# A fused attention and softplus feed-forward kernel: another list and order of the start, and strided scores of 54 rows in two lasting PSUM tiles

## The chip, the core and the metric

The kernel runs on one core of a Trainium2 chip. The metric is the device time of one execution in microseconds. TensorE (PE; its weight loads are listed as PEld) multiplies matrices into PSUM, VectorE (DVE), ScalarE (ACT) and GpSimd (POOL) work on elements, and SyncE (SP) issues most DMAs. The engines have a queue each and meet through semaphores.

## The reference

Eight batches of eight heads attend over 576 tokens of 64 dimensions; the first four heads see the last 32 keys, the other four the keys of their own class modulo 32. The result, as rows of 512 numbers, goes through a feed-forward layer with a softplus.

```python
scores = scale * np.matmul(q, k.transpose(0, 1, 3, 2))
mask_local = (rel >= 0) & (rel < stride)                    # heads 0 to 3
mask_strided = (rel >= 0) & (pos[None, :] % stride == pos[:, None] % stride)
attn = softmax(np.where(masks, scores, -1e9))
x = (attn @ v) as (4608, 512)
h = x @ w_in                                                # 512 -> 2048
g = np.maximum(h, 0.0) + np.log1p(np.exp(-np.abs(h)))
out = g @ w_out                                             # 2048 -> 512
```

The host reorders the strided heads so that the 18 tokens of a class lie side by side; a group of three classes is 54 tokens.

## The kernel before

**The feed-forward part.** The 4608 tokens are taken in nine chunks of 512 and the 2048 hidden channels in 16 slices f of 128, so there are 144 steps. A step has one *hidden* block on TensorE (`hidden`, L729): 12 matmuls of 128 x 128 by 512, since each of four pairs of heads gives three products, high part of x by high and by low part of w_in, and low part of x by high part. They add up in one PSUM bank. ACT takes absolute value, exponential and logarithm of it (`log_part`, L741 to L746), DVE adds the positive part (`softplus`, L750, tile `u`), which is the last reader of the bank, and splits the sum into a high and a low part (`gh` at L269, `gl` at L762). Two steps later an *output* block (`output`, L769) of 12 matmuls adds to four PSUM banks `py`, one for each 128 tokens. After the 16th slice `result` copies the four banks out and stores them.

**The attention part.** Two heads make a pair, in each batch in the order local, strided, local, strided; 32 pairs in all. The first four go through a form of their own at the start. Each of the other 28 has a *visit* on TensorE (`visit`): a row of small matmuls with its scores and with the weighted sums of the pair before it. The scores of a strided pair (`late_scores`, L422) are 22 products, 11 groups by two heads, which the profile lists as 44 loads and 44 matmuls. `lhsT` is 64 columns of q, the group's 54 and the first 10 of the next, so 64 rows of PSUM are written for each head; the rows of the surplus mean nothing. They fill two banks. `add_mask` (L533) reads the banks, and DVE and ACT make the softmax in SBUF (prob). Weighted sums are L475 for a local pair, L461 for a strided one, scores of local pairs L443.

**The banks.** PSUM has eight: four for `py`, one each in the pools `ps_s` and `ps_o`, and two in the pool `ps_h` with `bufs=2`. From `ps_h` come the banks of the hidden blocks, of the strided scores (both), of a third of the local scores and of the transposes in the start. The pool hands them out in turn, each after the last use of the tile that had it before.

**The order.** All is issued by hand. `FIRST` is a list of some 500 names that sets the order of the start: loads (q, k, v, wi, wo), scores S, maxima X, exponentials E, transposes T and their copies C, weighted sums V, copies into x (H, the high part) and differences (L, the low part), the preparation of the weights (a, B, d, h, l), the hidden blocks F and output blocks O of the first chunk, its softplus parts A, u, Gh, Gl, and the visits J4 to J8. W is a pair of matmuls without use that keep TensorE going. `ON_POOL`, `ON_VECTOR` and `ON_SCALAR` say which names run on another engine than the usual one, `WIDE` which halves of the first pairs take their exponential in one piece over SBUF, where the others take it in pieces of 64 columns straight from PSUM. Behind the list a planner (`Plan`) places the rest: each task has an urgency, an engine, a cost and tasks it follows; a task is put at the first gap of its engine after the end of what it follows, and all are issued in order of their start. There `F`, `O`, `S` and `Y` are hidden block, output block, visit and mask.

Of the kernel before, what the change touches and what calls it, by code (L numbers as in the profile page):

```python
# [44 lines left out]
ao0 v0 X10 hi0 r0 wi9 x10 R0 M0 S20 T02 Bo0 do0 C02 x11 v1 T00 T01 v2 S21 E10 wi1 X20 li0 E11 C01
C00 S30 ho0 V00 r1 Y20 X21 wi3 R1 x21 E20 S31 v3 V02 E21 Z20 wi2 M1 T11 X30 V01 X31 Y30 H00 q4 r2
C11 R2 L00 lo0 x31 T12 E30 M2 T10 H01 k4 Z30 L01 ai9 C12 E31 V11 T20 C10 Bi9 V12 wo6 V10 r3 T22 C20
H10 di9 T21 R3 L10 wo1 H11 wi4 C22 wo2 L11 M3 V22 C21 ai1 V20 V21 H20 Bi1 di1 T32 hi1 C32 H21 T31
wo3 ai3 L20 C31 L21 Bi3 T30 C30 V32 ai2 di3 li1 V31 V30 H30 H31 hi3 Bi2 wi6 L30 D4 L31 Fa0 di2 wi8
wo4 hi9 ao6 J4 Y42 Y40 v4 hi2 F0 li3 li2 W18 wi10 wi5 ao1 A0 Bo1 Y41 Ae0 Fa1 Al0 wi7 ai4 do1 q5 wo15  # L50
li9 Bo6 F1 wo8 u0 wi13 Gh0 ho1 Km A1 wo10 Bi4 lo1 Ae1 ao3 F2 Gl0 di4 wo5 Al1 hi4 O0 A2 do6 X4 u1 ho6
F3 lo6 ai6 Bi6 Gh1 li4 ao2 Ae2 s4 wo13 Bo2 Al2 Gl1 ai8 di6 Bo3 Bi8 do3 E4 u2 hi6 Z4 r4 do2 k5 ho3
di8 R4 li6 O1 Gh2 A3 Ae3 Al3 M4 F4 u3 Gl2 wi11 P41 ho2 lo2 Gh3 Gl3 F6 O2 A4 wi14 ai5 Ae4 wi12 P40
Al4 lo3 ai7 A6 hi8 P42 Bi5 ao4 Bi7 Kz di5 D5 u4 hi5 Ae6 P43 O3 Al6 u6 Gh4 Gh6 J5 v5 k7 di7 li8 li5
Bo4 ai11 ao5 Y51 wo14 Y50 F5 X5 H40 Gl4 wo7 hi7 Bi11 k6 do4 A5 s5 ho4 E5 Bo5 lo4 li7 Ae5 F9 Z5 ai10
wo11 r5 Al5 wo12 Gl6 di11 R5 wo9 q6 A9 Ae9 Bi10 O4 u5 ao8 di10 M5 do5 Gh5 Al9 hi11 hi10 u9 Gl5 F7
ho5 P53 A7 lo5 F8 H41 Bo8 L40 Ae7 Gh9 P51 ao7 Gl9 wi15 Al7 D6 O5 li10 A8 P50 do8 u7 P52 Ae8 ai12 O6
L41 ho8 Al8 Bo7 J6 u8 li11 v6 F10 Gh7 ai13 Y60 do7 Gh8 H51 Y61 lo8 Gl8 ho7 q7 Y62 X6 Bi12 lo7 H50
Gl7 F11 ao9 A10 di12 s6 ao10 Ae10 hi12 Bi13 Al10 Bo10 di13 u10 A11 O7 li12 E6 ai14 L50 hi13 F12 Z6
r6 Bo9 Ae11 do9 ho9 Bi14 R6 M6 Al11 do10 L51 li13 u11 D7 lo9 O8 Gh11 ho10 F13 ao13 Gh10 P60 Gl11 A12  # L60
O9 P62 di14 P63 Gl10 k8 hi14 Ae12 li14 P61 ao11 A13 Al12 lo10 u12 Ae13 Al13 Gh12 ao12 u13 ai15 Bo11
do11 J7 Bo12 Y71 do12 H61 Y70 O10 X7 Gh13 H60 v7 Gl12 Bo13 ho11 lo11 W23 s7 do13 E7 ho12 Bi15 F14 Z7
r7 A14 lo12 di15 R7 hi15 L61 L60 M7 ao15 li15 Ae14 q8 ho13 D8 P72 Al14 k9 P71 Gl13 lo13 P70 u14 O11
# [60 lines left out]
def attention_softplus_ffn(  # L124
# [406 lines left out]
    def add_mask(n, j):  # L531
        pv, sv, _ = parts(n, j)
        nc.vector.tensor_tensor(pv, sv, mask_of(n, j), op=ALU.add)  # L533
# [599 lines left out]
```

## Time and profile before

| | us |
|---|---|
| median of three runs | 878.86 (878.12 to 880.0) |
| the profiled execution | 880.72 |
| its span, first to last instruction | 878.9 |
| TensorE busy | 863.3 |
| DVE busy | 590.4 |
| ACT busy | 395.5 |

In a row of the page's groups or of the timeline stand line, engine, operation, tile written <- tiles read, shapes, and the time in us; in brackets the engine's idle time just before, and what ended it. In a row of the waits stand who waited, for whom, the total, how often and the longest. TensorE's granted clock is 0.998 of full speed over the span.

### The profile page before, as it was taken

The page shows a single profiled execution, that of the slowest core. Times are in us where ns is not written, and L with a number is a line of the kernel's source. Part 1 is how long each engine was busy: PE and PEld are TensorE (multiplying, and loading weights), DVE is VectorE, ACT ScalarE, POOL GpSimd, SP SyncE. Part 2 cuts the span into 40 slices and gives each one's busy share as a digit, 9 for nine tenths or more (in the row PEclk, how much of TensorE's full clock was granted, in tenths as well). Part 3 has the DMA queues.
Part 4 walks back from the last instruction along what each step waited for, and adds up shares of the span by engine and source line. Part 5 has one row for each costly group of instructions (what it writes and reads, how often), then busy time and mean ns, then how long its engine had stood idle before and what let it go on. Part 6 is the DMA issues. An engine that isn't in the chain of part 4 may idle for free.

```text
span 878.9 us, 16412 instructions
## 1 busy us (share of the span) xinstructions
PE 863.3 (98%) x6704; PEld 706.5 (80%) x6704; DVE 590.4 (67%) x1282; ACT 395.5 (45%) x703; POOL 75.4 (9%) x97
## 2 busy tenths in 40 slices
PE   7999999999999999999999999999999999999998
PEld 4788888888788878888788878888788888888886
DVE  5999968777876777768685867677776533333332
ACT  5877735444444443443444444344443333333332
POOL 4566650000000000000000000000000000000000
PEclk9999999999999999999999999999999999999999
DMA  9975103111210121102211121012100010001001
GB/s 305 345 274 188 48 14 103 49 50 43 90 42 22 49 75 42 43 28 56 76 43 42 43 90 43 15 47 85 41 16 16 1 48 1 1 1 48 1 1 48
DMA packets 46465, 56.46 MB, mean 64 GB/s; under 512 B 3322, under 2 KB 31670, under 8 KB 46390
## 3 DMA queue, kind: packets, MB, share of 16 engines
q1 hardware_dynamic: 46102, 55.09, 19.5%
q8 instruction: 52, 0.85, 0.4%
q10 hardware_dynamic: 288, 0.33, 0.2%
q14 instruction: 23, 0.19, 0.1%
HBM read 45.97 MB, written 9.44 MB: 63 GB/s over the span
## 4 chain that ended last, share of the span: by engine, by line
PE 95%; ACT 2%; DVE 2%; issue 1%; DMA 1%; SPq 0%; POOL 0%; DVEq 0%; ACTq 0%
PE ph L729 45%; PE py L769 44%; PE ps L422 1%; PE ps L461 1%; PE ps L443 1%; PE ps L475 1%; DMA early_h<-in_qk_dram 1%; DVE u L750 1%; ACT u L744 1%; ACT u L746 1%; ACT u L741 0%; PE pv L622 0%; PE py L393 0%; PE po L443 0%; PE po L461 0%
## 5 line engine op out<-in xcount | busy, mean ns | idle before, releaser
L769 PE MATMUL py<-w_o,gh 128*128 128x512 f32 x1152 | 357.8, 392 | 0.0
L729 PE MATMUL ph<-x_h,w_i 128*128 128x512 f32 x1152 | 355.6, 390 | 1.0 <-DVE prob L533 0.5
L741 ACT ACTIVATE u<-ph 128x512 f32<-128x512 f32 x144 | 86.1, 598 | 376.0 <-PE ph L729 375.7
L729 PEld LDWEIGHTS ph<-x_h,w_i 128*128 128x128 f32 x1152 | 215.6, 188 | 47.0 <-DVE u L750 1.1
L769 PEld LDWEIGHTS py<-w_o,gh 128*128 128x128 f32 x1152 | 214.3, 188 | 44.8
L769 PE MATMUL py<-w_o,gl 128*128 128x512 f32 x576 | 224.2, 389 | 0.0
L729 PE MATMUL ph<-x_l,w_i 128*128 128x512 f32 x576 | 224.1, 389 | 0.0
L750 DVE SCALAR_TENSOR_TENSOR u<-ph,u 128x512 f32<-128x512 f32 x144 | 99.2, 689 | 181.6 <-ACT u L746 180.1
L769 PEld LDWEIGHTS py<-w_o,gl 128*128 128x128 f32 x576 | 108.1, 188 | 22.7
L729 PEld LDWEIGHTS ph<-x_l,w_i 128*128 128x128 f32 x576 | 108.1, 188 | 22.6
L762 DVE TENSOR_TENSOR gl<-u,gh 128x512 fp32r<-128x512 f32 x135 | 93.4, 692 | 10.9 <-PE po L475 0.5
L746 ACT ACTIVATE u<-u 128x512 f32<-128x512 f32 x144 | 91.0, 632 | 4.3
L744 ACT ACTIVATE u<-u 128x512 f32<-128x512 f32 x144 | 91.0, 632 | 4.3
L592 DVE STREAM_TRANSPOSE masks_pt<-prob 32x160 f32<-32x160 f32 x224 | 70.1, 317 | 3.9
L269 DVE CAST gh<-u 128x512 fp32r<-128x512 f32 x129 | 54.6, 424 | 8.6 <-PE py L769 0.5
L580 DVE STREAM_TRANSPOSE pt_groups<-prob 32x192 f32<-32x192 f32 (+1 forms) x112 | 39.6, 354 | 3.1
L580 DVE STREAM_TRANSPOSE masks_pt<-prob 32x160 f32<-32x160 f32 (+1 forms) x112 | 39.6, 354 | 3.1
L548 ACT ACTIVATE prob<-prob 128x576 f32<-128x576 f32 (+1 forms) x28 | 19.4, 693 | 46.2 <-DVE prob L542 46.2
L269 ACT COPY qT<-prob 128x576 f32<-128x576 f32 x27 | 34.5, 1279 | 6.0 <-PE ps L422 5.2
L552 DVE TENSOR_REDUCE st<-prob 128x9 f32<-128x576 f32 (+1 forms) x28 | 21.2, 758 | 9.2 <-ACT prob L548 9.2
L533 DVE TENSOR_TENSOR prob<-ps,masks_pt 128x320 f32<-128x320 f32 (+1 forms) x28 | 10.8, 390 | 24.6 <-PE ps L443 14.5
L269 DVE COPY o<-py 128x512 f32<-128x512 f32 (+1 forms) x16 | 10.7, 670 | 16.9 <-PE py L769 16.9
(105 smaller groups left out, 587.1 us busy)
## 6 DMA issues: line engine op xcount, KB each, us to landing
out_dram<-o SPq DMA_DIRECT2D x35, 256.0 KB, 2.0
ri<-in_moe_w_in_dram SPq DMA_DIRECT2D x16, 512.0 KB, 9.8
ro<-in_moe_w_out_dram SPq DMA_DIRECT2D x16, 512.0 KB, 6.8
prob<-in_qk_dram SPq DMA_DIRECT2D x28, 288.0 KB, 2.8
kT<-in_qk_dram SPq DMA_DIRECT2D x28, 288.0 KB, 3.4
v_in<-in_v_dram SPq DMA_DIRECT2D x14, 162.0 KB
v_in<-in_v_dram SPq DMA_DIRECT2D x14, 160.0 KB, 3.1
v_in<-in_v_dram SPq DMA_DIRECT2D x14, 128.0 KB, 3.1
```

The costliest lines, as they stand in the source:

```text
L269: (engine.copy if engine is nc.scalar else engine.tensor_copy)(dst, src)
L548: nc.scalar.activation(pv, pv, AF.Exp, scale=SCALE)
L552: nc.vector.tensor_reduce(sm, pv, axis=AX.X, op=ALU.add)
L580: nc.vector.transpose(dst[:, :, :32], src[:, :, :32])
L592: nc.vector.transpose(pt_late[lo : lo + 32, h, windows, col : col + 32], src[:, :, 32 * c : 32 * c + 32],)
L729: nc.tensor.matmul(ph, lhsT=w32["i", f][:, half, cc * P : (cc + 1) * P], rhs=x_of(x, cc)[:, t0 : t0 + n], start=(i == 0), stop=(i == 3 * N ...
L741: nc.scalar.activation(us[c, f], phs[c, f], AF.Abs)
L744: nc.scalar.activation(u, u, AF.Exp, scale=-1.0)
L746: nc.scalar.activation(u, u, AF.Ln, bias=1.0)
L750: nc.vector.scalar_tensor_tensor(u, in0=phs.pop((c, f)), scalar=0.0, in1=u, op0=ALU.max, op1=ALU.add)
L762: engine.tensor_tensor(g, us.pop((c, f)), ghs[c, f].bitcast(F32), op=ALU.subtract)
L769: nc.tensor.matmul(py[t], lhsT=g[:, sl], rhs=w32["o", f][:, half], start=(f == 0 and n == 0), stop=(f == NFC - 1 and n == 2),)
```

## The change

The score products of strided pairs take 54 columns of q, so that they write 54 rows per head; the ten columns of zeros behind qT are cleared no longer. The pool of two turning PSUM buffers becomes two tiles that last for the whole kernel, `free_banks`. `take_bank` takes the one that was left first, and `leave_bank` gives it back, at the softplus, at the added mask and at the copy of an early transpose. In the planner, a task may follow another with a lead, and the visit of a strided pair now follows, besides what it did, the softplus of its step with a lead of 0.7 and the output block two steps back. The list and its tables are new.

```diff
@@ FIRST, the first of its lines @@
-mask k0 q0 wi0 W q1 S01 ai0 X01 k1 S00 wo0 x01 X00 S11 x00 q2 W19 S10 k2 k3 E01 Bi0 q3 E00 X11 di0
+mask k0 q0 k1 W S01 q1 wi0 S00 q2 k3 X01 x01 k2 X00 S11 E01 wo0 ai0 x00 S10 q3 wi1 E00 X11 X10 v0 v1
...
 WIDE = """
-20 30
+21 30
 """.split()
@@ Plan.run @@
-            after = [a for a in after if a in self.tasks]
-            for a in after:
+            after = [a if isinstance(a, tuple) else (a, 0.0) for a in after]
+            after = [(a, lead) for a, lead in after if a in self.tasks]
+            for a, _ in after:
                 place(a)
-            t = max([end[a] + self.WAIT for a in after], default=0.0)
+            t = max([end[a] + self.WAIT - lead for a, lead in after], default=0.0)
@@ the banks @@
-    ps_h = ctx.enter_context(tc.tile_pool(name="ps_h", bufs=2, space=bass.MemoryType.PSUM))
+    ps_h = ctx.enter_context(tc.tile_pool(name="ps_h", bufs=1, space=bass.MemoryType.PSUM))
+    free_banks = [ps_h.tile([P, 512], F32, name=f"ph{i}") for i in range(2)]
+    held = {}
+    def take_bank(key):
+        held[key] = free_banks.pop(0)
+        return held[key]
+    def leave_bank(key):
+        free_banks.append(held.pop(key))
@@ group_masks @@
-        nc.gpsimd.memset(qT[:, S:], 0.0)
@@ late_scores @@
-            pss[n, part] = ps_h.tile([P, 512], F32, tag="ph", name=f"ps_{n}_{part}")
+            pss[n, part] = take_bank(("s", n, part))
...
-                        pss[n, part][to : to + 64, j : j + GROUP],
-                        lhsT=qT[head, c : c + 64],
+                        pss[n, part][to : to + GROUP, j : j + GROUP],
+                        lhsT=qT[head, c : c + GROUP],
@@ add_mask @@
         pss.pop((n, j))
+        if ("s", n, j) in held:
+            leave_bank(("s", n, j))
@@ early_transposes, early_copy, hidden, softplus: take_bank and leave_bank likewise @@
...
@@ the visits in the planner @@
         after += [f"P{n-1}", f"v{n-1}", f"u{i-1}"]
+        if not is_local(n):
+            after += [(f"u{i}", 0.7), f"O{i-LAG}"]
```

Three places show how the order moves. The first is TensorE at the start of the third chunk, from the end of a hidden block into a strided pair's visit. In rows of before, `ph_2` is the bank of the hidden block, `py_108` to `py_111` are the four output banks, and `ps`, `po` take the weighted sums.

```order
L729 MATMUL ph_2_3707<-x_h_583,w_i_659 128x512 x2
L729 MATMUL ph_2_3707<-x_l_591,w_i_659 128x512
L769 MATMUL py_108<-w_o_385,gh_0_3677 128x512 x2
L769 MATMUL py_108<-w_o_385,gl_0_3679 128x512
L475 MATMUL ps_3734<-masks_pt,v_in 64x64 x2
L475 MATMUL po_3735<-masks_pt,v_in 64x64 x2
```

In the changed kernel the same place on TensorE reads (L745 is the hidden block, L786 the output block, L488 the weighted sums, `ph_113` one of the lasting banks):

```order
L745 MATMUL ph_113<-x_h_606,w_i_567 128x512 x2
L745 MATMUL ph_113<-x_l_608,w_i_567 128x512
L786 MATMUL py_108<-w_o_492,gh_0_3604 128x512 x2
L786 MATMUL py_108<-w_o_492,gl_0_3606 128x512
L786 MATMUL py_109<-w_o_492,gh_0_3604 128x512 x2
L786 MATMUL py_109<-w_o_492,gl_0_3606 128x512
L786 MATMUL py_110<-w_o_492,gh_0_3604 128x512 x2
L786 MATMUL py_110<-w_o_492,gl_0_3606 128x512
L786 MATMUL py_111<-w_o_492,gh_0_3604 128x512 x2
L786 MATMUL py_111<-w_o_492,gl_0_3606 128x512
L488 MATMUL ps_3670<-masks_pt,v_in 64x64 x2
```

The other nine matmuls of the output block, which stood behind the visit, now stand ahead of it; it is so at the start of five chunks, and behind the start of the program TensorE's blocks and visits keep their order otherwise.

The second place is ACT in the start, around the exponentials of the third and fourth pair. `early_l_98` and `early_l_100` are these pairs' probabilities, `x_h` is the high part of x, `a_i` and `a_o` are weights in preparation, the copies move transposed probabilities out of PSUM. Before:

```order
L503 ACTIVATE early_l_98<-early_l_98 128x6x64
L521 ACTIVATE early_l_98,st_351<-py_109,st_351 128x64 x3
L663 CAST x_h_440<-pv_0_387 128x288
L503 ACTIVATE early_l_100<-early_l_100 128x6x64
L663 CAST x_h_440<-pv_1_388 128x288
L689 ACTIVATE a_i_464<-ri_278 128x512
L521 ACTIVATE early_l_100,st_432<-py_111,st_432 128x64 x3
L269 COPY masks_pt<-pt_0_476 128x4x96
```

In the changed kernel ACT's queue reads there:

```order
L534 ACTIVATE early_l_98,st_326<-py_108,st_326 128x64 x6
L705 ACTIVATE a_i_404<-ri_260 128x512
L516 ACTIVATE early_l_98<-early_l_98 128x3x64
L283 COPY masks_pt<-ph_113 128x4x96
L283 COPY masks_pt<-ph_112 128x4x96
L516 ACTIVATE early_l_100<-early_l_100 128x6x64
L534 ACTIVATE early_l_100,st_412<-py_111,st_412 128x64 x3
L679 CAST x_h_458<-pv_0_429 128x288
L283 COPY early_h_99<-ph_113 128x384
```

Both exponentials of the fourth pair now stand ahead of the first copy into x and of a weight step; the third pair takes six of its nine pieces from PSUM where it took three.

The third place is DVE ahead of the first strided visit, from the transposes of the first late pair to that visit's mask. `u_4` and `u_6` are the softplus sums of two hidden blocks, and the rows with `mask_g` add the mask. Before:

```order
L693 TENSOR_SCALAR a_i_892<-a_i_892 128x512
L693 TENSOR_SCALAR a_i_903<-a_i_903 128x512
L700 SCALAR_TENSOR_TENSOR a_i_892<-ri_668,a_i_892 128x512
L750 SCALAR_TENSOR_TENSOR u_4_888<-ph_4_834,u_4_888 128x512
L592 STREAM_TRANSPOSE masks_pt<-prob 32x5x32 x2
L592 STREAM_TRANSPOSE masks_pt<-prob 32x4x32 x2
L750 SCALAR_TENSOR_TENSOR u_6_905<-ph_6_863,u_6_905 128x512
L700 SCALAR_TENSOR_TENSOR a_i_903<-ri_688,a_i_903 128x512
L693 TENSOR_SCALAR a_o_914<-a_o_914 128x512
L533 TENSOR_TENSOR prob<-ps_1_972,mask_g 128x270
```

In the changed kernel the queue of DVE reads:

```order
L766 SCALAR_TENSOR_TENSOR u_6_847<-ph_113,u_6_847 128x512
L607 STREAM_TRANSPOSE masks_pt<-prob 32x5x32 x2
L607 STREAM_TRANSPOSE masks_pt<-prob 32x4x32 x2
L766 SCALAR_TENSOR_TENSOR u_4_887<-ph_112,u_4_887 128x512
L709 TENSOR_SCALAR a_i_895<-a_i_895 128x512
L709 TENSOR_SCALAR a_i_889<-a_i_889 128x512
L716 SCALAR_TENSOR_TENSOR a_i_889<-ri_776,a_i_889 128x512
L546 TENSOR_TENSOR prob<-ph_113,mask_g 128x324
```

The last softplus ahead of the visit now follows the other one after four transposes, with two weight steps less around it, and belongs to another hidden block. On TensorE the visit then stands behind one output block where it stood behind two, and ahead of an output block where a hidden block followed at once.

More of the change, by code (lines that the diff above doesn't have):

```diff
@@ L43 @@
 FIRST = """
-mask k0 q0 wi0 W q1 S01 ai0 X01 k1 S00 wo0 x01 X00 S11 x00 q2 W19 S10 k2 k3 E01 Bi0 q3 E00 X11 di0
[L45 to L63, printed above, removed]
@@ L64 @@
-O12 F15 Bo15 A15 O13 P73 Ae15 Al15 J8 Gh14 u15 ao14 Bo14 H70 do14 H71 L71 L70 Qa0 Gl14 q9 Gh15 Q0
-do15 ho15 QA0 ho14 lo14 O14 Gl15 Qu0 Q1 lo15 QA1 Ob15 O15 y1 Qu1 Qh0 y2 Qh1 y0 v8 y3 Ql0 Ql1
+mask k0 q0 k1 W S01 q1 wi0 S00 q2 k3 X01 x01 k2 X00 S11 E01 wo0 ai0 x00 S10 q3 wi1 E00 X11 X10 v0 v1
+x10 r0 wi3 v2 E10 x11 E11 Bi0 R0 wi2 ao0 M0 W15 S20 X20 T01 S21 di0 x20 E20 v3 S30 wo1 S31 hi0 r1
+T00 C01 ai1 Bo0 R1 X21 Y21 k4 q4 X30 wi4 X31 E21 li0 Y30 C00 T02 Z21 wi6 x31 M1 V00 do0 r2 C02 Bi1
+E30 E31 T11 wi9 V02 R2 Z30 V01 H00 M2 C11 L00 wo2 T10 T12 H01 C10 C12 L01 T21 V10 r3 ai3 wo3 R3 M3
@@ new lines @@
+ho0 Bi3 V12 lo0 C21 V11 H10 L10 T22 H11 wi12 L11 T20 C20 wi8 C22 ai2 V21 V20 V22 T30 H20 T31 W23 W17
+di1 C30 di3 wo6 L20 Bi2 H21 L21 di2 T32 hi3 hi2 V30 C31 C32 V31 hi1 ao1 V32 Bo1 Km li3 Fa0 H30 L30
+H31 L31 D4 li2 v4 do1 J4 li1 Y40 ai4 F0 ho1 Bi4 ai6 A0 Ae0 q5 Fa1 F1 wi10 Al0 Y42 Y41 ai9 X4 di4 lo1
+u0 s4 hi4 Gh0 wi14 A1 Bi9 E4 Bi6 Gl0 F3 Ae1 Al1 O0 di6 di9 hi6 ao3 u1 Kz F2 li4 A3 wo15 ao2 k5 Bo3
+wo13 Ae3 li6 ao6 wo4 wi5 hi9 Gh1 Al3 Gl1 li9 Z4 ai8 u3 Bi8 Bo6 r4 di8 F6 wi7 wo8 A2 Bo2 Ae2 do2 R4
@@ new lines @@
+Al2 O1 M4 do3 u2 W18 wo11 hi8 Gh3 ho3 ho2 Gh2 D5 Gl3 A6 Ae6 wo9 do6 ho6 wo5 Gl2 P43 lo2 wo7 F4 P40
+P42 Al6 A4 ai5 Ae4 lo3 u6 Al4 ai7 P41 u4 li8 Bi7 q6 ai10 lo6 Gh4 Bi5 O2 Gh6 J5 di5 Y50 wo10 hi5 di7
+ao4 li5 Bo4 O3 Y51 X5 hi7 li7 Bi10 s5 F5 do4 E5 wi11 ho4 di10 Gl4 v5 k6 Z5 F9 H41 Gl6 ao7 H40 A5 Bo7
+ao5 Ae5 A9 Al5 lo4 r5 Bo5 ao9 R5 M5 do5 L40 wi15 Ae9 O4 u5 Al9 wo14 L41 do7 F7 ho5 Gh5 u9 ho7 P52
+Gl5 lo5 A7 hi10 Ae7 P53 Gh9 P50 Al7 u7 F8 lo7 Gl9 ai12 wi13 D6 ai11 O5 P51 Gh7 Bo9 Bi11 di11 J6 Y60
@@ new lines @@
+O6 Bi12 do9 A8 Y62 Y61 hi11 li10 ho9 ao8 X6 Bo8 di12 s6 Ae8 hi12 E6 li11 F10 do8 Gl7 O7 Al8 li12 v6
+Z6 u8 r6 ho8 A10 R6 M6 lo8 Gh8 ai13 Ae10 P61 Al10 Gl8 F11 A11 u10 k7 ao10 wo12 Bi13 Ae11 F12 di13
+ai14 lo9 Gh10 W19 O8 hi13 ao11 Gl10 P62 Al11 H50 li13 ai15 P60 u11 A12 Bo10 F13 Ae12 Gh11 q7 k8 D7
+O9 Bi14 H51 Bi15 Al12 Gl11 Bo11 di14 hi14 P63 A13 L51 Ae13 do10 L50 u12 Al13 u13 ho10 lo10 ao12 W21
+do11 J7 ho11 di15 Bo12 Y71 H61 O10 H60 li14 hi15 li15 lo11 ao15 Gh13 do12 v7 Gh12 q8 F14 ho12 Y70
@@ L66 @@
+ao13 X7 Gl12 Gl13 Bo13 F15 s7 do13 E7 O11 A14 Z7 L60 r7 Ae14 ho13 Al14 R7 lo12 A15 u14 L61 M7 Ae15
+ao14 P70 O12 D8 P72 lo13 Al15 P73 Gh14 P71 Bo14 O13 u15 J8 k9 do14 H71 Gl14 Gh15 ho14 L71 H70 Qa0
+lo14 q9 L70 Q0 Bo15 do15 ho15 QA0 Gl15 v8 Qu0 lo15 O14 Q1 Qh0 QA1 Ob15 Qu1 O15 y3 y1 y2 Qh1 y0 Ql1
+Ql0
 """
 ON_POOL = """
-x00 hi0 r0 x10 x11 x21 x31 r3 hi1 hi9 ho1 hi4 hi8 hi7 r5 hi10 ho5 Gh7 hi13 r6 hi14 ho11 r7 Gh14 ho14
+x01 x00 x10 r0 hi0 r1 r3 hi3 hi1 ho1 hi4 hi9 r4 r5 ho5 Gh5 Gh9 r6 ho8 Gh10 hi13 hi14 r7 ho15
@@ L70 @@
 """.split()
 ON_VECTOR = """
-M0 C02 li0 C11 C12 C10 C21 C32 li1 hi3 li2 lo1 Gl0 lo6 Gl1 Gl2 Gl4 lo4 Gl6 lo7 Gl7 Gl12 lo12 hi15 D8
-Gh15 ho15
+M0 C01 C10 M3 ho0 hi2 li2 li1 Gl0 li4 li6 Gh1 li9 li5 Gl4 Gl6 M6 lo9 lo10 lo11 Gl12 Gl13 lo12 ho14
+Gl15 lo15
 """.split()
@@ L597, in early_transposes @@
     def early_transposes(n, t):
-        ph = ps_h.tile([P, 512], F32, tag="ph", name=f"pt_{n}_{t}")[:, : 4 * TILE]
+        ph = take_bank(("t", n, t))[:, : 4 * TILE]
         phs["t", n, t] = ph = ph.rearrange("p (a h c) -> p a h c", a=2, h=2)
@@ L612, in early_copy @@
         copy_on(engine, pt_of(n, t), src)
+        leave_bank(("t", n, t))
     def early_weighted(n, t):
@@ L722, in hidden @@
         if 0 in pairs:
-            phs[c, f] = ps_h.tile([P, 512], F32, tag="ph", name=f"ph_{c}_{f}")[:, :n]
+            phs[c, f] = take_bank((c, f))[:, :n]
         ph = phs[c, f]
@@ L752, in softplus @@
         )
+        leave_bank((c, f))
     def g_high(c, f, engine=nc.vector):
```

## The prediction

> **What bounds the kernel now.** I read the page's busy shares first, then the chain that ended last, then the waits of TensorE, then the timeline around one of those waits.
>
> ```profile
> PE 863.3 (98%) x6704; PEld 706.5 (80%) x6704; DVE 590.4 (67%) x1282; ACT 395.5 (45%) x703; POOL 75.4 (9%) x97
> PE 95%; ACT 2%; DVE 2%; issue 1%; DMA 1%; SPq 0%; POOL 0%; DVEq 0%; ACTq 0%
> 40.29 2.72 PE py L769 x12
> PE ps L422 <- DVE u L750: 5.3, 5, 1.1
> ```
>
> TensorE is busy 98% of the span and holds 95% of the chain that ended last. Its unit of work is a block of 12 matmuls of 512 columns, 2.72 us or 0.227 us a matmul (third row, from the chain). There are 288 such blocks (144 of L729, 144 of L769), 783 us of the 878.9 us span, and the change touches none of them. What is left is some 95 us: the start before the first block, the 28 visits of the attention, the end, and waits. The largest wait of TensorE is the last row: five times, 1.06 us each, the strided scores of L422 wait for the softplus sum `u` of L750 on DVE. The five sit where a new chunk of tokens begins. This is one of them, from the timeline:
>
> ```profile
> 326.86 0.60 ACT L741 ACTIVATE u<-ph 128x512 f32<-128x512 f32 x1 [2.55 <-PE ph L729]
> 328.81 0.69 DVE L750 SCALAR_TENSOR_TENSOR u<-ph,u 128x512 f32<-128x512 f32 x1 [2.96 <-ACT u L746]
> 328.20 0.29 PE L422 MATMUL ps<-kT,qT 64*64 64x54 f32 x4
> 329.56 0.80 PE L422 MATMUL ps<-kT,qT 64*64 64x54 f32 x40 [1.06 <-DVE u L750]
> 330.29 0.73 PE L769 MATMUL py<-w_o,gh 128*128 128x512 f32 x2
> 150.70 0.87 PE L422 MATMUL ps<-kT,qT 64*64 64x54 f32 x44
> 151.50 0.50 PE L769 MATMUL py<-w_o,gh 128*128 128x512 f32 x1
> ```
>
> The scores need both banks. The second is still read by the softplus of the hidden block just computed; DVE gives it up at 328.81 + 0.69 = 329.50, and TensorE goes on at 329.56. So the 44 pieces take 330.29 - 328.20 = 2.09 us. The last two rows are an ordinary strided visit: 151.50 - 150.70 = 0.80 us, no wait. The difference, 1.29 us, holds the idle time and a restart of the row of matmuls.
>
> **The order at a chunk's start.** With the added dependences a strided visit stands behind the whole output block, not behind its first quarter. Nine matmuls of 0.227 us, 2.04 us, slide ahead of it. The scores would then begin at 328.20 + 2.04 = 330.24, and the bank is free at 329.50: 0.7 us to spare. The matmuls that slide ahead must themselves be ready. They write the output banks, which the copies of the last chunk have to leave:
>
> ```profile
> 325.17 0.68 DVE L269 COPY o<-py 128x512 f32<-128x512 f32 x1
> ```
>
> The last copy ends at 325.85, before the visit at either place. Behind the scores, DVE's chain of the softmax starts 2.04 - 1.29 = 0.75 us later, but there are then as many blocks between this visit and the next (seven) as at the ordinary ones, where nothing waits. The q, k and v loads issued after the visit move with it and are needed a visit or more later, 20 us, against about 3 us to land. So five times 1.29 us go and nothing is late next: **-6.45 us**. I see no other place behind the start where TensorE's order changes.
>
> **54 rows instead of 64.** Each strided product loads 54 columns of q, not 64; what it streams, 54 columns of k, stays.
>
> ```profile
> L422 PEld LDWEIGHTS ps<-kT,qT 64*64 64x64 f32 x616 | 11.6, 135 | 6.0 <-DVE u L750 6.0
> L443 PEld LDWEIGHTS ps<-kT,qT 64*32 64x32 f32 x784 | 10.1, 105 | 4.9 <-issue 4.2 <-ACT qT L269 0.4 <-DVE masks_pt L580 0.4
> 171.67 0.26 PE L461 MATMUL ps<-pt_groups,v_in 54*64 54x54 f32 x1
> 172.51 0.50 PE L769 MATMUL py<-w_o,gh 128*128 128x512 f32 x1
> ```
>
> The row of 616 loads is 14 visits of 44. A load of 64 columns takes 135 ns, one of 32 takes 105, so 0.94 ns a column: ten columns less are 9.4 ns, 7% of a load. If loads pace the row of 44, a visit saves 7% of 0.80 us, 0.056 us, 14 times 0.8 us. If the streamed columns pace it, nothing. The other end comes from the nearest odd shape: L461, with 54 rows in the contraction, takes 172.51 - 171.67 = 0.84 us for its 44 pieces, 0.04 more than L422; if 54 costs that much here, +0.6 us. No run has this shape. The short loads of L443 are the nearer row, since they vary just what changes, and I take **-0.8 us**. The ends are -1.75 (0.80 us shrunk in proportion to the columns, 10 / 64 of it, 14 times) and +0.6.
>
> By the Trainium skill (TensorE: Matmul & The Clock Gate, "LDWEIGHTS") a load's time goes by its columns at 1.2 per ns, 8.3 ns for ten; the slope of the two rows, 0.94 ns a column, agrees, though the durations as a whole are over twice the page's. Against that, the skill's TensorEngine Tiling ("Instruction Overhead") says that a dimension that is already small brings nothing, a matmul of one column taking as long as one of 60; applied to this dimension, this term would be 0 and the sum 0.8 us higher.
>
> **The new list and its order.** The list moves nearly every piece of the first 120 us, DMA loads, preparation of weights and POOL's and DVE's shares among them. The amounts hardly change: ACT gains three 64-column exponentials, four copies and one q layout, DVE loses five copies and gains three differences, TensorE gets four more warming matmuls. What counts is when the first block starts. These are ACT's and TensorE's rows:
>
> ```profile
> 7.80 0.30 ACT L521 ACTIVATE early_l<-py,st 128x64 f32<-128x64 f32 x1
> 8.09 0.31 ACT L521 ACTIVATE early_l<-py,st 128x64 f32<-128x64 f32 x1
> 15.29 0.86 ACT L269 COPY masks_pt<-pt 128x384 f32<-128x384 f32 x2 [0.72 <-PE pt L604]
> 20.86 0.40 ACT L663 CAST x_h<-pv 128x288 fp32r<-128x288 f32 x1 [2.88 <-PE pv L622]
> 22.36 0.40 ACT L663 CAST x_h<-pv 128x288 fp32r<-128x288 f32 x1 [0.69 <-PE pv L622]
> 22.66 0.68 ACT L689 ACTIVATE a_i<-ri 128x512 f32<-128x512 f32 x1
> 23.82 0.32 ACT L521 ACTIVATE early_l<-py,st 128x64 f32<-128x64 f32 x1
> 25.07 0.70 ACT L663 CAST x_h<-pv 128x288 fp32r<-128x288 f32 x2 [0.18 <-PE pv L622]
> 27.33 0.70 ACT L663 CAST x_h<-pv 128x288 fp32r<-128x288 f32 x2 [0.55 <-PE pv L622]
> 29.12 1.23 PE pv L622 x24
> 30.28 0.74 PE L729 MATMUL ph<-x_h,w_i 128*128 128x512 f32 x2
> ```
>
> Before, ACT sits idle for 2.88 us up to 20.86: on TensorE the last scores of the fourth pair stand behind the first pair's transposes and products, and on ACT the first pair's copy into x stands ahead of the fourth pair's exponentials, which end at 23.82 + 0.29 = 24.1. Now both come first. From the first exponential at about 7.6 us ACT has 27 pieces at 0.29 (the step from 7.80 to 8.09), three weight steps of 0.58 (22.66 to the next piece), two wide exponentials of together 0.8 and two copies of together 0.75: 11.1 us, and with the 0.6 us that ACT waited among its exponentials before, 19.3 us. Then come six copies into x at 0.31, eight transposed copies at 0.38 and two weight steps, 6.1 us, and waits for TensorE as before, 0.69 + 0.18 + 0.55 = 1.4: 26.8 us. The last products of the fourth pair take 1.23 us (last but one row), so the first block starts at about 28.0, not 30.28: -2.3 us. Without any of those waits it would be 26.0, so -4.3 is the far end; no gain at all is the near one.
>
> After it, at the first strided visit, TensorE lost half a microsecond:
>
> ```profile
> 54.01 0.58 ACT L741 ACTIVATE u<-ph 128x512 f32<-128x512 f32 x1
> 58.40 0.69 DVE L750 SCALAR_TENSOR_TENSOR u<-ph,u 128x512 f32<-128x512 f32 x1
> 61.45 0.70 PE L729 MATMUL ph<-x_h,w_i 128*128 128x512 f32 x2 [0.54 <-DVE prob L533]
> ```
>
> A hidden block followed the visit at once and had to wait until the mask was added and a bank free (last row). Now an output block of 2.72 us comes between: -0.5 us. The price may come ahead of the visit: only one output block, 2.72 us, and the products, 0.78 us, now separate it from the last hidden block, where there were two. Softplus took from 54.01 to 59.09, 5.1 us, through the crowded queues of ACT and DVE; as slow again, the scores would wait 5.1 + 0.1 - 3.5 = 1.7 us. In the new order DVE has only one pair of transposes between the two sums, and ACT's q layout stands ahead of the softplus, so I leave this at nothing. The start in all: **-2.8 us**, ends -4.8 and +1.7.
>
> The lasting tiles take the two banks in the order in which they are left, as the pool did in turn, so I cost them at nothing: the waits on a bank are for the same readers.
>
> **The sum.** The profiled execution took 880.72 us, 1.8 more than its span. 880.72 - 6.45 - 0.8 - 2.8 = 870.67. The median of the runs shown, 878.86, lies 1.86 below that execution, so I expect 868.8. The ends are 878.86 - 6.45 - 1.75 - 4.8 = 865.9 and 878.86 - 6.45 + 0.6 + 1.7 = 874.7.
>
> **Rivals.** *The start gives it back.* For 80 us after the first 20, DVE is nearly full:
>
> ```profile
> 0.00:20.00 20.00, 16.13 (x342) 9.96 (x342) 9.25 (x23) 11.05 (x50) 8.08 (x29) 0.91 0.94 309
> 20.00:40.00 20.00, 18.03 (x217) 13.77 (x216) 18.79 (x42) 16.39 (x36) 10.57 (x17) 1.00 1.01 332
> 80.00:100.00 20.00, 20.00 (x197) 16.46 (x196) 19.19 (x43) 14.84 (x27) 12.70 (x12) 1.00 0.16 48
> ```
>
> The third figure of each row is DVE: 9.25 us of the first 20, 18.79 of the next, 19.19 at 80 to 100. If TensorE starts earlier and DVE doesn't, TensorE meets waits for weights and softplus further on, and the 2.8 us come back, with up to 1.7 of the first visit on top: 871.6 to 873.3, say 872.5. For it speaks that the DMA is full too (0.94 and 1.01 of its time, about 320 GB/s), and that the weights of slice 5 move from 13.0 MB to 15.7 MB in the order of loads, through at some 49 us for a use at some 57 (28.0, ten blocks and two visits). Against it: DVE's 10.75 idle microseconds in the first 20 are room for the work that moves up.
>
> *The wait stays.* There are still two banks, and if the change moved the visits without reaching the bank's release, the 6.45 us would stay: 868.8 + 6.45 = 875.3. The rows speak against it: release and new start are 0.7 us apart. The Trainium skill (Perfetto Trace Analysis, "Optimization Strategy") reads a gap that repeats on the saturated engine as a possible lack of SBUF or PSUM, and by that a third bank would be the cure, not an order; here the wait is for a bank, as the page has it, but the release lies within reach of the nine matmuls.
>
> *Slower: 54 columns break the packing.* L422 runs four 64 by 64 pieces side by side, which is how 44 loads of 135 ns fit in 0.80 us. If 54 columns can't be packed so, the 44 follow each other at 135 ns, 5.9 us, 5.1 more a visit, 14 times 72 us: 868.8 + 0.8 + 72, about 942. It decides from (6.45 + 2.8) / 14 = 0.66 us more a visit on, so if the row of 44 takes over 1.46 us. Against it speaks L461, whose 54 rows are packed at 0.84 us.
>
> **How the numbers follow.** The forecast has 0.60, the start that gives it back 0.25, the wait that stays 0.06, broken packing 0.05; 0.04 is for a list that loses over 5 us somewhere, half of it no change and half slower. Differences within 0.2%, 1.8 us, a measurement of this kernel can hardly tell from no change. Faster: 0.60 + 0.25 + 0.06 = 0.91, of which I leave 0.01 to no change; no change 0.03; slower 0.07. The range takes the ends, 865.9 to 874.7, rounded outwards: 865.5 to 875.0.
>
> **What would show it.** The row of TensorE's waits for L422 on DVE is gone, and every strided row of 44 takes 0.75 to 0.80 us. The loads of that line have 54 columns and some 125 ns. The first matmul of L729's successor starts near 28 us, and ACT's idle time of 2.88 us ahead of the first copy into x is smaller. If the row of 44 exceeds 1 us, or a wait on DVE for a hidden block of over 1 us appears in the first 120 us, or the first block starts later than 30, I am wrong in that step.

## The result and the profile after

The changed kernel takes 870.31 us (median of four runs, 869.64 to 870.83), the kernel before in the same runs 879.35 (878.12 to 880.0): a ratio of 0.9898, 95% interval 0.9881 to 0.9916. The forecast was 868.8, its range 865.5 to 875.0.

This is the profile of the changed kernel: the page's busy shares, the chain that ended last by engine, and from the waits three of the rows of TensorE (total, times, longest).

```profile
PE 859.6 (99%) x6708; PEld 704.4 (81%) x6708; DVE 589.5 (68%) x1281; ACT 398.8 (46%) x715; POOL 71.8 (8%) x91
PE 97%; ACT 1%; DMA 1%; POOL 0%; DVE 0%; SPq 0%; issue 0%; DVEq 0%; ACTq 0%
PE idle L809 <- DVE room L231: 1.2, 1, 1.2
PE py L388 <- ACT early_l L534: 1.2, 1, 1.2
PE ph L745 <- DVE u L766: 0.2, 1, 0.2
```

The row that led the waits before, the strided scores on DVE's `u` with 5.3 us, has gone, and no row of TensorE's waits takes its place: the longest is now 1.2 us. (Lines have moved: the strided scores are L435, hidden and output block L745 and L786, `u` is L766.) The third chunk's start, from the timeline of the changed kernel:

```profile
324.23 0.69 DVE L766 SCALAR_TENSOR_TENSOR u<-ph,u 128x512 f32<-128x512 f32 x1 [2.96 <-ACT u L762]
325.66 0.78 PE L435 MATMUL ph<-kT,qT 64*54 64x54 f32 x44
```

`u` leaves the bank at 324.23 + 0.69 = 324.92, and the scores begin at 325.66: 0.74 us to spare where before they stood 1.06 us idle. From their first piece to the next block all fourteen strided rows now take 0.71 us. Before there were eight of 0.80, one of 1.41 and five of 2.09. The loads have become a little shorter (groups by line), and the first hidden block begins at 28.09 us (timeline):

```profile
L435 PEld LDWEIGHTS ph<-kT,qT 64*54 64x54 f32 x616 | 9.8, 127 | 0.0
18.39 0.48 ACT L534 ACTIVATE early_l<-py,st 128x64 f32<-128x64 f32 x1
19.09 0.40 ACT L679 CAST x_h<-pv 128x288 fp32r<-128x288 f32 x1
28.09 0.74 PE L745 MATMUL ph<-x_h,w_i 128*128 128x512 f32 x2
```

ACT ends the fourth pair's exponentials near 18.7 us (18.39 and the step of 0.29) and goes on to the first copy into x at 19.09. The 2.88 us that it waited there before are gone.

### The profile page after: what moved, and what is told of

Read it like the earlier page. It is cut to its first block, busy times and chain, and to the rows that moved or that the text cites. A ratio compares the mean times of both kernels' runs of the same rounds, so it can differ in the third digit from the quotient of the medians.

```text
span 868.3 us, 16396 instructions
## 1 busy us (share of the span) xinstructions
PE 859.6 (99%) x6708; PEld 704.4 (81%) x6708; DVE 589.5 (68%) x1281; ACT 398.8 (46%) x715; POOL 71.8 (8%) x91
## 4 chain that ended last, share of the span: by engine, by line
PE 97%; ACT 1%; DMA 1%; POOL 0%; DVE 0%; SPq 0%; issue 0%; DVEq 0%; ACTq 0%
PE py L786 45%; PE ph L745 45%; PE ps L488 1%; PE ps L474 1%; PE ph L435 1%; DMA ri<-in_moe_w_in_dram 1%; PE ph L456 1%; PE pv L638 1%; ACT early_l L534 1%; PE ps L456 0%; PE ph L619 0%; PE po L456 0%; PE po L474 0%; PE po L488 0%; ACT a_i L705 0%
## 5 line engine op out<-in xcount | busy, mean ns | idle before, releaser
L786 PE MATMUL py<-w_o,gh 128*128 128x512 f32 x1152 | 357.9, 392 | 0.0
L745 PE MATMUL ph<-x_h,w_i 128*128 128x512 f32 x1152 | 355.5, 390 | 0.3 <-DVE u L766 0.2
L745 PEld LDWEIGHTS ph<-x_h,w_i 128*128 128x128 f32 x1152 | 215.8, 188 | 46.5 <-DVE u L766 1.0
L786 PEld LDWEIGHTS py<-w_o,gh 128*128 128x128 f32 x1152 | 214.1, 188 | 44.7
L745 PE MATMUL ph<-x_l,w_i 128*128 128x512 f32 x576 | 224.1, 389 | 0.0
L786 PE MATMUL py<-w_o,gl 128*128 128x512 f32 x576 | 224.1, 389 | 0.0
L766 DVE SCALAR_TENSOR_TENSOR u<-ph,u 128x512 f32<-128x512 f32 x144 | 99.1, 688 | 182.7 <-ACT u L762 181.2
L786 PEld LDWEIGHTS py<-w_o,gl 128*128 128x128 f32 x576 | 108.2, 188 | 22.6
L745 PEld LDWEIGHTS ph<-x_l,w_i 128*128 128x128 f32 x576 | 108.1, 188 | 22.4
L595 DVE STREAM_TRANSPOSE pt_groups<-prob 32x160 f32<-32x160 f32 (+1 forms) x112 | 39.6, 354 | 3.0
L679 ACT CAST x_h<-ps 128x288 fp32r<-128x288 f32 (+5 forms) x34 | 11.8, 366 | 24.5 <-PE po L488 20.1
```

The source lines that it names most:

```text
L595: nc.vector.transpose(dst[:, :, :32], src[:, :, :32])
L745: nc.tensor.matmul(ph, lhsT=w32["i", f][:, half, cc * P : (cc + 1) * P], rhs=x_of(x, cc)[:, t0 : t0 + n], start=(i == 0), stop=(i == 3 * N ...
L766: nc.vector.scalar_tensor_tensor(u, in0=phs.pop((c, f)), scalar=0.0, in1=u, op0=ALU.max, op1=ALU.add)
L786: nc.tensor.matmul(py[t], lhsT=g[:, sl], rhs=w32["o", f][:, half], start=(f == 0 and n == 0), stop=(f == NFC - 1 and n == 2),)
```

## The experiments: the wait

The change has four parts: the planner's rule, the lasting tiles, the 54 columns, the new list. The theory was that the rule alone takes the wait away, that the tiles are worth nothing, and that list and columns add their own terms. The first three kernels add the parts one by one, up to the changed kernel, and the fourth takes the columns back out of it. Lasting tiles without the rule weren't tried (a bank must be left, in program order, before it is taken, and the old order takes it before), nor 54 columns without the tiles (the mask would read rows that nothing has written).

**The rule alone**, on the kernel before:

```diff
-            after = [a for a in after if a in self.tasks]
+            after = [a if isinstance(a, tuple) else (a, 0.0) for a in after]
...
+        if not is_local(n):
+            after += [(f"u{i}", 0.7), f"O{i-LAG}"]
```

> The kernel before with one edit: in the planner a strided visit is entered behind u of its own block and behind the output block of two blocks earlier. Theory (the order alone removes the wait): the five S rows of 2.09 us become 0.80, the wait of the scores on DVE's u is gone from the waits, and the time is 879.35 - 5 x 1.29 = 872.9 us (872.3 to 873.5). Rival (two lasting tiles, or the narrower scores, remove it): the five rows stay at 2.09 and the time stays at 879.35. The first visit, at 120 us, comes from the list and keeps its 1.41.

872.96 us against 879.0 for the kernel before (six and 17 runs), ratio 0.9929 (0.9916 to 0.9942). This is its timeline at the third chunk's start:

```profile
326.53 0.69 DVE L751 SCALAR_TENSOR_TENSOR u<-ph,u 128x512 f32<-128x512 f32 x1 [2.96 <-ACT u L747]
327.96 0.87 PE L423 MATMUL ps<-kT,qT 64*64 64x54 f32 x44
328.76 0.73 PE L770 MATMUL py<-w_o,gh 128*128 128x512 f32 x2
```

The scores begin 0.74 us after the bank is free and take 328.76 - 327.96 = 0.80 us, with the pool's two turning buffers and 64 columns. The rule is enough. (The row that keeps its 1.41 us is the first strided visit, at 59 us in this trace, not at 120.)

**The rule and the lasting tiles:**

```diff
-            pss[n, part] = ps_h.tile([P, 512], F32, tag="ph", name=f"ps_{n}_{part}")
+            pss[n, part] = take_bank(("s", n, part))
```

> The planner's edit as in e1_planner, and with it the two lasting tiles of PSUM in place of the pool's turns, scores still 64 columns wide, list still that of before. Theory (the tiles by themselves are worth nothing, for the same instructions wait for the same ones): the time of e1_planner, 872.9 us by forecast, within 0.5 us of it. Rival (the pool's release costs waits that the lasting tiles don't have): 1 us or more below e1_planner.

872.92 us, 0.04 below the rule alone. The runs of either kernel lie more than 2 us apart, so the traces say it better: from the start of the first hidden block behind the first strided visit to the end of TensorE's last matmul, 807.40 us against 807.45. The tiles are worth nothing by themselves; they are what lets 54 rows stand in a bank whose other rows were written earlier.

**Rule, tiles and 54 columns, with the list of before** (the changed kernel with the old list and tables, of which this is the first line):

```diff
-mask k0 q0 k1 W S01 q1 wi0 S00 q2 k3 X01 x01 k2 X00 S11 E01 wo0 ai0 x00 S10 q3 wi1 E00 X11 X10 v0 v1
+mask k0 q0 wi0 W q1 S01 ai0 X01 k1 S00 wo0 x01 X00 S11 x00 q2 W19 S10 k2 k3 E01 Bi0 q3 E00 X11 di0
```

> The changed kernel with the list and the tables of engines of before: the planner, the lasting tiles and the 54 columns without the new start. Theory: below e3_banks by 14 rows of 0.09 us, 1.26 us, so 871.6 us, and S rows of 0.71 us. Against the changed kernel (870.31) it is later by what the new list is worth, 2.3 to 2.9 us, which gives 872.6 to 873.2; the two sums differ by 1 to 1.6 us and this run says which holds. Rival (narrower scores gain nothing, and the 0.80 to 0.71 in the trace of after comes from the new list): S rows of 0.80 and the time of e3_banks.

871.33 us (four runs), ratio 0.9915 (0.9901 to 0.9928): 1.59 below the last kernel. Thirteen rows take 0.71 us, the first 1.33. The first of the two sums held, and by it the new list is worth 871.33 - 870.31 = 1.02 us, not the 2.3 to 2.9 that I had read from the two traces.

**The changed kernel with 64 columns:**

```diff
-                        lhsT=qT[head, c : c + GROUP],
+                        lhsT=qT[head, c : c + 64],
```

> The changed kernel with score products that are again 64 columns wide (the columns of zeros are back in the transposed queries). Theory (the row's length goes by the columns that are loaded): S rows of 0.80 us instead of 0.71, 14 x 0.09 = 1.26 us more than the changed kernel in the same rounds, 871.6 us. Rival (the columns are hidden behind the streams of four row groups): rows of 0.71 and the time of the changed kernel, 870.3.

871.79 us, 1.48 above the changed kernel, rows of 0.80. Behind the first strided visit the traces have 807.15 us against 805.68. The ten columns are worth 1.5 us, seen from both sides.

**How much must stand ahead of the scores.** Two kernels change the dose. The first is the kernel before with six output matmuls ahead, where it had three and with the whole rule twelve:

```diff
+            after += [(f"u{i}", 1.4)]
```

> The kernel before with the planner's allowance alone, and a larger one: six of the twelve output matmuls stand ahead of the scores at the five chunk starts, where before has three and e1_planner twelve. Theory (the wait ends at a fixed time behind the hidden block, and each group of three matmuls ahead takes 0.68 us off it): S rows of 2.09 - 0.68 = 1.41 us at five places, so 5 x 0.61 = 3.05 us more than e1_planner (872.96), 876.0 us. Rival (the wait goes only where the whole block is ahead, or u ends later too as the order changes): rows of 2.09 and 879 us.

```profile
325.64 0.69 DVE L751 SCALAR_TENSOR_TENSOR u<-ph,u 128x512 f32<-128x512 f32 x1 [2.96 <-ACT u L747]
325.72 0.29 PE L423 MATMUL ps<-kT,qT 64*64 64x54 f32 x4
326.39 0.80 PE L423 MATMUL ps<-kT,qT 64*64 64x54 f32 x40 [0.39 <-DVE u L751]
327.12 0.73 PE L770 MATMUL py<-w_o,gh 128*128 128x512 f32 x2
```

This is its timeline. The idle time is 0.39 where it was 1.06, and the row takes 327.12 - 325.72 = 1.40 us, within 0.01 of the forecast. From the first hidden block behind the first strided visit to TensorE's last matmul this trace has 810.42 us, the rule alone 807.45, before (its second trace, below) 813.78. So from three to six matmuls ahead each of the five places gains 0.67 us, about the length of three matmuls (0.68), and from six to twelve the 0.59 that was left. The whole time, 874.83 (ratio 0.9955, 0.9942 to 0.9967), is 1.2 below the forecast; the next part shows where that comes from. The second has nine ahead, in the changed kernel:

```diff
-            after += [(f"u{i}", 0.7), f"O{i-LAG}"]
+            after += [(f"u{i}", 0.7)]
```

> The changed kernel without the planner's rule that a strided visit stands behind the output block; the rule on u, with its allowance of 0.7 us, stays. At the chunk starts nine of the twelve output matmuls then stand ahead of the scores and three behind. In the trace of after the bank is read to its end by u 2.0 us after the hidden block's end, and nine matmuls take 2.04 us. Theory (what counts is how much PE has ahead of the scores, not that the block is whole): S rows of 0.71 to 0.85 us and the time of the changed kernel, within 0.5 us. Rival (the allowance is too large on the chip, with the semaphore's delay the scores wait): S rows of 1.0 us or more at five places, 1.5 us or more above.

870.57 us, no difference from the changed kernel, and all rows 0.71 us: six matmuls beyond the first three are enough.

## The experiments: the start

**The list alone**, on the kernel before (the diff of the last list the other way round):

```diff
-mask k0 q0 wi0 W q1 S01 ai0 X01 k1 S00 wo0 x01 X00 S11 x00 q2 W19 S10 k2 k3 E01 Bi0 q3 E00 X11 di0
+mask k0 q0 k1 W S01 q1 wi0 S00 q2 k3 X01 x01 k2 X00 S11 E01 wo0 ai0 x00 S10 q3 wi1 E00 X11 X10 v0 v1
```

> The kernel before with the new list and its tables alone. Theory: the first hidden block begins at 28.1 us instead of 30.28, the block behind the first strided visit some 2.5 to 2.8 us sooner, the five S rows stay at 2.09, and the time is 879.35 - 2.7 = 876.6 us (876.0 to 877.2). Rival (what the start gains is given back before the steady part): 878.5 or more, with the first hidden block at 28.1 all the same.

877.98 us (11 runs), ratio 0.9993 (0.9985 to 1.0002): 1.0 us by the medians and hardly told from nothing. Yet its first hidden block begins at 27.86 us. It isn't the rival either: behind the first strided visit this trace has 813.61 us, the second trace of before 813.78, so nothing is given back. What was wrong was the start that I had compared it with.

**The kernel before once more**, with no edit:

> The kernel before once more, for another trace of its start. In its first trace the granted clock was 0.66 between 15 and 20 us and the first hidden block began at 30.28 us; in e3_banks and f1_oldlist, which have its list, the clock was 1.00 there and the block began at 28.81 and 28.92. Theory (1.3 to 1.5 us of the first trace's start is that stretch, not the list): at a clock of 1.00 to 30 us the first hidden block begins at 28.8 to 29.0 and the time is near 878.3. Rival (the list of before needs 30.28 with its own planner): 30.1 to 30.4 at a clock of 1.00.

879.3 us, 1.0 above the time expected; the block came where it was expected. The windows of five microseconds hold the answer. The last three figures of a row are granted clock, DMA share and GB/s; this is the trace of before on which the prediction was built:

```profile
15.00:20.00 5.00, 5.00 (x121) 3.61 (x120) 2.65 (x9) 2.69 (x10) 2.57 (x3) 0.66 0.99 294
```

And the same kernel's second trace:

```profile
15.00:20.00 5.00, 4.38 (x127) 3.21 (x125) 3.54 (x11) 3.27 (x12) 2.86 (x5) 1.00 1.08 348
28.94 0.72 PE L729 MATMUL ph<-x_h,w_i 128*128 128x512 f32 x2
60.07 0.70 PE L729 MATMUL ph<-x_h,w_i 128*128 128x512 f32 x2 [0.54 <-DVE prob L533]
```

At full clock the kernel before begins its first hidden block at 28.94 us, not 30.28, and the block behind the first strided visit at 60.07, not 61.45. A row of 48 score products inside that stretch tells the same, first trace first:

```profile
16.46 1.51 PE L393 MATMUL py<-early_h,raw_q 64*32 64x64 f32 x48
16.08 0.95 PE L393 MATMUL py<-early_h,raw_q 64*32 64x64 f32 x48
```

At the start of the stretch the first trace is 0.11 us behind the second, at its end 1.43. Some 1.35 us of the first trace's start were a stretch of low clock that some executions have and others don't. The trace of the changed kernel with 64 columns has one too (0.67 between 10 and 15 us), and its first hidden block begins at 29.09 instead of 28.09. Of the 17 runs of before in the first experiments, the five with a mean clock of 0.998 took 879.68 to 880.31 us and the twelve with 1.000 took 878.01 to 879.22. The profiled execution, at 880.72, was one of the former kind.

A second piece of the old start was a stop of TensorE in the middle of a row of eight products, one that the prediction had not looked at. From the timeline of this second trace of before:

```profile
18.99 0.39 PE L622 MATMUL pv<-masks_pt,room 128*64 128x96 f32 x4
20.58 0.39 PE L622 MATMUL pv<-masks_pt,room 128*64 128x96 f32 x4 [1.21 <-issue]
```

"issue" means that the engine waited for nothing that the profile shows. The kernel with six matmuls ahead has the same list, and the same eight products go through:

```profile
18.58 0.55 PE L623 MATMUL pv<-masks_pt,room 128*64 128x96 f32 x8
```

Five of the six traces with the old list have the stop, at the same product, 1.1 to 1.5 us long; the sixth is this one. For its profiled execution that covers the 1.2 us by which its time fell short of the forecast. None of the seven traces with the new list, or with one changed from it, has the stop in these products.

This sixth trace also shows what the new order on ACT brings by itself. These are its last exponential of the fourth pair and its first hidden block:

```profile
21.16 0.33 ACT L522 ACTIVATE early_l<-py,st 128x64 f32<-128x64 f32 x1
27.81 0.72 PE L730 MATMUL ph<-x_h,w_i 128*128 128x512 f32 x2
```

The exponentials end at 21.16 + 0.29 = 21.45 us, 2.8 us later than in the changed kernel, and the first block begins at 27.81 all the same, where the changed kernel has 28.09. Behind the first strided visit the two are equal, 58.96 and 58.95. So up to there the new list is ahead of the old one, in these traces, only by the old one's stop. What stops the old one, the view of the DMA queues suggests. In windows of 1 us, a packet of the instruction queue q8 shows at 18 to 19 us in the second trace of before:

```profile
q8 instruction: 1, 0.02, 5.5%
```

and at 16 to 17 us in the trace without the stop. The other four with the stop have it at 17 to 19, the changed kernel at 15 to 16. That instructions came late is thus likely, not shown: no experiment moved that packet alone, and why one trace of the old list has it sooner stays open.

**More weights out of the way.** Two further kernels tried to improve the changed list. In the first, ACT's `ai1` and `ao0` and what hangs on them go behind the fourth pair's exponentials, `ai0` behind those of the first pair, and POOL's `li0` behind M1:

```diff
-wo0 ai0 x00 S10 q3 wi1 E00 X11
+wo0 x00 S10 q3 wi1 E00 ai0 X11
...
-M2 C11 L00 wo2 T10 T12 H01 C10 C12 L01 T21 V10 r3 ai3 wo3 R3 M3
+M2 C11 L00 wo2 T10 T12 H01 C10 C12 L01 T21 V10 r3 ai3 ao0 wo3 R3 Bo0 M3
```

> The changed kernel with its list changed once more at the start: of the preparation of weights, the scaling of the first input weights goes behind the exponentials of the first pair, POOL's low part of them (1.28 us ahead of the second pair's normalisation, for which PE waits 0.7) goes behind that normalisation, and the scaling of the second input weights and the first output weights (0.82 and 0.78 us on ACT between exponentials) go behind the fourth pair's exponentials with what follows them. Theory (the start is paced by ACT's exponentials, then by the copies and products that follow): exponentials end some 1.2 us sooner, near 17.5 us, and the first hidden block begins 0.5 to 1.2 us sooner; time 869.1 to 869.8. Rival (the low part, now at 16 to 18 us, or the weights moved make PE, POOL or the copies late later): no gain or up to 1 us lost.

872.05 us, 1.7 above the changed kernel, the first hidden block at 30.66. From the waits of TensorE and DVE's timeline of this kernel:

```profile
PE pv L638 <- DVE x_l L677: 2.3, 3, 1.4
19.61 0.43 DVE L709 TENSOR_SCALAR a_i<-a_i 128x512 uint32<-128x512 uint32 x1 [1.86 <-ACT a_i L705]
```

The weight step that follows the moved `ai1` stood, in DVE's queue, ahead of the third pair's reciprocal and held DVE for 1.86 us; further weight steps then stood ahead of the differences for which TensorE waits. Nor did the exponentials end sooner (near 18.9 us), as ACT now waited for transposes. The second kernel keeps only `ai0` and `li0` moved:

```diff
-wo0 ai0 x00 S10 q3 wi1 E00 X11
+wo0 x00 S10 q3 wi1 E00 ai0 X11
...
-E21 li0 Y30 C00 T02 Z21 wi6 x31 M1 V00
+E21 Y30 C00 T02 Z21 wi6 x31 M1 li0 V00
```

> The changed kernel with two of g2_weights' moves alone: the scaling of the first input weights behind the exponentials of the first pair, POOL's low part of them behind the second pair's normalisation. In g2_weights the normalisation ended 1.3 us sooner by this (15.99 us against 17.33), and the weighted products after it began at 17.42 against 17.37 all the same. Theory (another chain, of transposes and copies, is as late): no change, 870.3 us within 0.4. Rival (what g2_weights lost hid a gain): 0.4 to 1.2 us less.

870.01 us (869.79 to 871.12), ratio 0.9900 (0.9884 to 0.9915): no change, as the theory had it. The products that the second pair's normalisation was thought to hold back begin at 17.27 us, against 17.37 in the changed kernel. In both traces that is 0.7 us behind the start of ACT's copy of their transposes (16.57 and 16.65), so it is this copy that they follow. No version here beats the changed kernel by more than its runs differ.

## The experiments: what a column costs

The last kernel is the changed one with 32 columns of q in the strided scores. It leaves out the scores of the other 22 queries of each group.

```diff
-                        pss[n, part][to : to + GROUP, j : j + GROUP],
-                        lhsT=qT[head, c : c + GROUP],
+                        pss[n, part][to : to + 32, j : j + GROUP],
+                        lhsT=qT[head, c : c + 32],
```

> The changed kernel with only the first 32 of each group's 54 queries in the strided score products; the other 22 rows of scores keep what the bank held, so this part of the scores is left out. Theory (0.80 to 0.71 us for ten columns is 0.009 us a column all the way down): S rows of 0.51 us, 14 x 0.20 = 2.8 us less than the changed kernel, 867.5 us. Rival (below some width the streamed rows or the issue of 44 matmuls sets the pace): S rows of 0.6 to 0.71 us, 868.8 to 870.3.

871.71 us: 1.4 slower than the changed kernel, outside both expectations. Its rows take 0.69 to 0.70 us, against 0.71. These are the rows of one visit, loads first, with 64 columns:

```profile
100.95 0.80 PEld L436 LDWEIGHTS ph<-kT,qT 64*64 64x64 f32 x44
101.00 0.87 PE L436 MATMUL ph<-kT,qT 64*64 64x54 f32 x44
101.81 0.50 PE L787 MATMUL py<-w_o,gh 128*128 128x512 f32 x1
```

with 54 (the changed kernel), with the weighted sums' last pieces ahead:

```profile
99.81 0.70 PEld L435 LDWEIGHTS ph<-kT,qT 64*54 64x54 f32 x44
99.82 0.22 PE L488 MATMUL po<-masks_pt,v_in 64*64 64x64 f32 x2
99.86 0.78 PE L435 MATMUL ph<-kT,qT 64*54 64x54 f32 x44
100.57 0.73 PE L786 MATMUL py<-w_o,gh 128*128 128x512 f32 x2
```

and with 32:

```profile
99.80 0.62 PEld L435 LDWEIGHTS ph<-kT,qT 64*32 64x32 f32 x44
99.65 0.23 PE L488 MATMUL po<-masks_pt,v_in 64*64 64x64 f32 x2
99.81 0.77 PE L435 MATMUL ph<-kT,qT 64*32 64x54 f32 x44
100.50 0.73 PE L786 MATMUL py<-w_o,gh 128*128 128x512 f32 x2
```

Four pieces run side by side, and a new four begins every 58 ns with 64 columns, every 50 with 54 and, past the first two, every 48 with 32, by the starts of the loads. So the pace goes by the loaded columns from 64 to 54, 0.8 ns a column; at that rate four of 32 would start every 32 ns, but something holds them at 48. Whether that is the 54 streamed columns of k or the issue, no run tells. And there is a new cost. With 54 columns the first load starts beside the last products of the weighted sums, 99.81 against 99.82; with 32 it starts at 99.80 against 99.65, when these are well under way. The row of weighted sums ahead of the scores then lasts 0.89 us instead of 0.78, at all 14 visits: 14 x 0.11 = 1.5 us, which covers the loss. Why the narrower load waits, no run here tells.

## Why the prediction was right, and where not

- **The bound.** TensorE's own work was the bound and has stayed it: 99% busy, 97% of the chain.
- **The wait, -6.45 us.** Right in place, mechanism and size. The rule alone brought 6.0 us by the medians and 813.78 - 807.45 = 6.3 by the traces. The margin, 0.7 us as forecast, was 0.74, and nothing became late next.
- **The lasting tiles, nothing.** Right: 0.04 us.
- **54 columns, -0.8 us.** The mechanism was right, the size too small: 1.5 us. I took the saving from how long a single load lasts, 7%. But a load overlaps the others, and what counts is how often four can start: 58 to 50 ns, 14%, near the end of -1.75 that I had put down for a time in proportion to the columns. Besides the 0.09 us of the row, the output block behind it took 0.02 less.
- **The start, -2.8 us.** This step failed, in its first term: "so the first block starts at about 28.0, not 30.28: -2.3 us". 30.28 was not what the kernel before does at full clock, which is 28.94, and the gain is 0.85. Of ACT's wait of 2.88 us, on which the term was built, the second trace of before has 1.55. The number 28.0 came true (28.09; the exponentials ended near 18.7, forecast 19.3), but the path to it did not: in the one trace with the old list and no stop the exponentials end at 21.45 and the first block begins at 27.81, so it isn't the exponentials that set it. What the list gained ahead of the first block is no more than the stop of 1.1 to 1.5 us that its traces don't have. That the stop doesn't occur with the new list was not foreseen: what gain there was came by luck. With the first strided visit, where some 0.3 of the forecast 0.5 us came, and what follows, the start is worth 60.07 - 58.95 = 1.1 us up to the block behind that visit and 0.26 later (805.94 us from that block on with the old list, 805.68 with the new), 1.4 in all by the traces and 1.0 by the medians. The loss feared at that visit (1.7) didn't come, as the timeline of the changed kernel shows:

```profile
54.52 0.69 DVE L766 SCALAR_TENSOR_TENSOR u<-ph,u 128x512 f32<-128x512 f32 x1 [0.58 <-ACT u L762]
55.41 0.78 PE L435 MATMUL ph<-kT,qT 64*54 64x54 f32 x44
58.95 0.62 PE L745 MATMUL ph<-x_h,w_i 128*128 128x512 f32 x2
```

`u` leaves the bank at 55.21, the scores begin at 55.41, and the hidden block at 58.95 waits for nothing.
- **The same 1.4 us were counted twice.** The sum took 1.86 us off because the profiled execution lay above the median, and took the late start of that very execution off again as the list's gain. A row that the prediction quotes for DVE says so: 0.91 is the granted clock of the first 20 us. I used its DVE column and passed over the clock.
- **The sum.** By the traces at full clock, spans 877.5 and 868.3: 6.3 + 0.05 + 1.5 + 1.4 = 9.2 us, forecast 10.05. Too much for the start and too little for the columns cancelled in part, which is luck. By the medians it is 879.35 - 870.31 = 9.0. So of the 1.5 us by which 868.8 fell short, 1.0 is in the terms and 0.5 in the median taken as the base, 878.86 from three runs.
- **The rivals.** *The start gives it back* (872.5) lay further from the time than the forecast did, and its mechanism didn't occur: nothing was given back. *The wait stays* and *broken packing* fall with the rows of 0.71 us. What was uncertain lay in the baseline, and no rival covered that.

By the Trainium skill (TensorEngine Tiling, "Instruction Overhead") a matmul of one free column takes as long as one of 60, and no tiling factor is to be taken from a dimension that is already small. The prediction applied this to the loaded columns, of which the page doesn't speak: there the rows agree between 54 and 32 (0.71 and 0.70 us) and disagree between 64 and 54, where ten columns brought 1.5 us in all. The gap that repeats on the saturated engine, which the Trainium skill (Perfetto Trace Analysis, "Optimization Strategy") reads as a possible lack of PSUM, closed here with the same two banks, as the rule alone shows.

## What to carry to other kernels

Where a saturated engine waits a fixed time for a buffer, count the independent work that can stand ahead of the wait: here each piece moved ahead took its own length off, until the wait was used up, and no further buffer was needed. Before a gain is read from one profiled execution, look at the granted clock of the very stretch that it comes from and at stops that no releaser explains, and don't correct for the median and for the stretch both. Price a shortened small matmul by how often a new one starts in its row, not by how long one load lasts.

## What the hardware showed that was not expected

- A granted clock of 0.66 over five microseconds of the start, in some executions, cost some 1.35 us in the start of the first trace of before, and shows in the whole only as a mean of 0.998 instead of 1.000.
- TensorE stopped for 1.1 to 1.5 us in the middle of a row of equal products, with no releaser, in five of six traces of one list; a packet of the instruction queue shows 1 to 2 us later in those than in the sixth.
- Score loads of 32 columns behind loads of 64 waited 0.11 us for the row ahead, where loads of 54 or 64 columns did not, and so cost more than they saved.
